# Top-k attention and an MLP mixer on one core: a threshold scaled inside the list pass, a ninth tile's columns copied with its group's, and two smaller moves

## The chip, the cores and the metric

The kernel runs on one core of a Trainium2 chip. The metric is the device time of one execution in microseconds (us). The core has five engines that run side by side, each with its own list of instructions in a fixed order: TensorE (PE, with its weight loads as PEld), VectorE (DVE), ScalarE (ACT), GpSimd (POOL) and SyncE (SP), which here only issues transfers. On one engine an instruction waits for everything ahead of it; between engines they wait on semaphores.

## The reference

For 8 batches and 8 heads, with 576 rows of 64 columns each, attention keeps for each row only the scores that are not below its 32nd largest:

```
scores = scale * q @ k.T                       # 576 x 576 a head
kth    = 32nd largest of each row
scores = where(scores >= kth, scores, -1e9)
attn   = exp(scores - max) / (sum + 1e-9)
x      = attn @ v                              # heads side by side: 576 x 512 a batch
```

Then comes an MLP mixer on each batch: `h = relu(x.T @ w_tok1) @ w_tok2`, `u = x + h.T`, and the output `u + relu(u @ w_ch1) @ w_ch2`.

## The kernel before

**Units.** The work is cut into 32 pairs of heads, counted from 0 (four pairs a batch). A pair has 1152 score rows: nine tiles of 128 rows, where the ninth holds the last 64 rows of both heads. The tiles form two groups, the first of four tiles, the second of five. The columns of a tile are 512 and a tail of 64.

**Scores.** `qk_tr` (L323) transposes q and k on TensorE, `qk_ev` copies them to the tile qkT. `s1_mm` (L358) multiplies for the tail columns of a group's four whole tiles into two PSUM banks (one for each head), and `s1_ev` (L377) copies them to the score tile SS; `s0_mm` and `s0_ev` (L384, L398) do the 512 columns. The ninth tile has its own pair of functions, `st_mm` and `st_ev` (L401, L415), called once for the 512 columns and once for the 64. Nearly all these copies are ScalarE's.

**The 32nd largest.** VectorE finds it group by group, and this is its main work:

- `upper` (L426) takes the larger of columns i and i+288 into `hi`; `split4` (L447) splits these lists again, into `lo` and `hx` (L452, L456, L460).
- four rounds of `top_round` (L465): MAX8 on each tile's list (L473), then MATCH_REPLACE8 (L478, each with a MATCH_VALUE_LOAD) in the first three;
- GpSimd meanwhile makes the list of the smaller elements by integer arithmetic: `both_bits` (L433, an addition) and `lower_bits` (L441, a subtraction), each 128 x 1152 elements;
- **the list pass**, `low_round` (L489): one MAX8 a tile on `lo` (L492), with a TENSOR_REDUCE (L483) behind the first. Its last element of each tile is the threshold, in column KTH+7 of the tile A.

**The mask.** There are two ways. For tiles 0 and 1 of each group ("turned" tiles; none in the last pair's second group), `raise_kth` (L541) scales the thresholds of the whole group by 2^90 into the tile kbig (a TENSOR_SCALAR on VectorE, L544). ScalarE's `steep` (L547) makes from it a tile U that is large below the threshold, GpSimd's `sink` (L556) subtracts U from the scores in SS (L558, two a group), ScalarE's `expo` exponentiates, and a transposing transfer turns the result. For the other tiles ScalarE makes U from the unscaled threshold (`below_act`, L565), and TensorE's transposing products subtract it. In the last pair's second group VectorE masks the tiles itself (`kept`, L572). GpSimd also copies a few columns of A aside for a final check (`keep_ends`, L496, two short copies, L500 and L501), makes the negated maxima (`neg_max`, L515) and issues the loads of v and of the weights.

**The output of attention.** `o_mm` (L644) multiplies the turned probabilities with v and a column of ones; `o_den` (L659) takes the reciprocal of the sums on VectorE (L662); for the second head of odd pairs VectorE multiplies by it at once (`o_ev_dve`, L679, at L681), in the other cases ScalarE does (`o_ev`, L665). Then come the mixer's steps (`h1_mm` to `out_ev`), and for the last batch a longer ending (`plan_part_sums`, `plan_mlp_last`): sums over three quarters of the channels made ahead, kept in free tiles, and joined with the last pair's.

**The order.** No loop nest sets the order. `plan_unit` (L856), `plan_mlp` and the two functions for the last batch give each piece of work to a planner (`Plan`, L40) with an engine, an assumed duration, a priority (often from the table RANK, L20), what it depends on and which buffers it takes. `Plan.order` (L66) plays these through, always starting the task of lowest priority number that is ready, and the instructions are then written in that order on every engine. A task that moves can so shift others. Tasks marked `port` (all of GpSimd's, `upper` and `split4`) exclude each other in the plan; `raise_kth` is not marked. Where TensorE would idle, `spare` (L271) adds multiplications that nothing reads.

In `plan_unit` the scaling is a task of its own behind the list pass:

```python
y = add("FREE", 0.0, 0, lambda: None, deps=[kd[g]])
kb = add("DVE", 0.07, U - 1100, lambda g=g: raise_kth(st, g), deps=[y], acq=[("kbig", u, g)], slack=0.2)
m = add("ACT", 0.67, V + RANK["steep" + str(g)] + i, lambda i=i: steep(st, i), deps=[kb, chain.get("steep")], acq=[("U", u, i)])
```

The zero-length task of the engine "FREE" lets VectorE pick another task first.

Of the kernel before, what the change touches and what calls it, by code (L numbers as in the profile page):

```python
# [19 lines left out]
RANK = {  # L20
    "begin_l": -2054, "o_wait": 16, "t_wait": 6, "q_wait": 272, "v_wait": 112, "pre_mm": -34365, "pre_ev": -31279, "rest_mm": 14920,
    "begin": 31546, "flags": 8794, "rush": -6145, "rush6": -3394, "load": -9078, "qk_tr": 7627, "qk_ev": -3163, "st_mm": -8007,
    "st_ev": 896, "keep": 3463, "h1_mm": -30213, "h1_ev": 3666, "ut_mm": -46945, "ut_ev": -3088, "out_mm": 13329, "out_ev": -772,
# [125 lines left out]
def kernel(  # L149
# [138 lines left out]
    def load_one(st, name, src, b, p, queue=None):  # L288
# [11 lines left out]
        queue.dma_start(  # L300
            out=t[0:TAIL, NT, :, :], in_=rws[:, W:S, :].rearrange("h p c -> p h c")
        )
        st[name] = t
# [41 lines left out]
    def qk_tail_tr(st, kind="tp"):  # L345
        tails = bank(kind)[:, 0 : 2 * TAIL].rearrange("p (i c) -> p i c", i=2)
        for i, name in enumerate("qk"):
            nc.tensor.transpose(
                tails[:, i, :],
                st[name][0:TAIL, NT, :, :].rearrange("p h d -> p (h d)"),  # L350
                identF[0:TAIL, 0:TAIL],
            )
        st["tails"] = tails
# [4 lines left out]
    def s1_mm(st, g, kind="s0"):  # L358
        T = st["T"]
        x = [bank(kind) for hh in range(2)]  # L360
        for a in range(4):
            t, hh = 2 * g + a // 2, a % 2
            nc.tensor.matmul(
                out=x[hh][:, (a // 2) * TAIL : (a // 2 + 1) * TAIL],
                lhsT=T[rows[hh], 0, t * P : (t + 1) * P],
                rhs=T[rows[hh], 1, W:S],
                start=True,
                stop=True,
            )
        st["s1"] = x  # L370
# [30 lines left out]
    def st_mm(st, part):  # L401
        T = st["T"]
        lo, hi = ((0, W), (W, S))[part]
        x = bank("s0")
        for hh in range(2):
            nc.tensor.matmul(
                out=x[hh * TAIL : (hh + 1) * TAIL, 0 : hi - lo],
                lhsT=T[rows[hh], 0, W:S],
                rhs=T[rows[hh], 1, lo:hi],
                start=True,  # L410
                stop=True,
            )
        st["st", part] = x

    def st_ev(st, part):  # L415
        lo, hi = ((0, W), (W, S))[part]
        nc.scalar.copy(out=st["SS", 1][:, 4, lo:hi], in_=st.pop(("st", part))[:, 0 : hi - lo])
# [71 lines left out]
    def low_round(st, g):  # L489
        n, A = 4 + g, st["A", g]  # L490
        for i in range(n):
            nc.vector.max(A[:, i, KTH : KTH + 8], st["lo"][:, i, :])  # L492
            if i == 0:
                both_low(st, g, n - 2, n)

# [44 lines left out]

    def raise_kth(st, g):  # L541
        x = m8p.tile([P, NS], f32, name="kbig", tag="kbig")
        n = 4 + g
        nc.vector.tensor_scalar_mul(x[:, 0:n], st["A", g][:, 0:n, KTH + 7], STEEP)  # L544
        st["kbig", g] = x
# [310 lines left out]
    def plan_unit(u):  # L856
# [6 lines left out]
        for name, src in (("q", q), ("k", k)):  # L863
            aside = u < 2 and name == "k"
            ld[name] = add("ACT" if aside else "SP", 1.75, U - 5000 if aside else U + RANK["load"],
                           lambda name=name, src=src, aside=aside: load_one(st, name, src, b, p, nc.scalar if aside else None),
                           acq=[("ld" + name, u)])
        ev, prev = [], None
        for i in range(2):
            a = add("PE", 0.61, U + RANK["qk_tr"], lambda i=i: qk_tr(st, i), deps=[ld["qk"[i]], prev] + chain.get("first", []), acq=[("tp", u, "q", i)] + ([] if i else [("qkT", u)]), slack=(3.0 if u == 0 else 4.5) if u < 5 else 0.1 * RANK["q_wait"])  # L870
# [18 lines left out]
        for g in range(2):  # L889
            early = u == 0 and g == 0  # L890
            kind = "mps" if early else "s0"
            a = add("PE", 0.65, U + RANK["s_mm" + str(g)] + 10 * g, lambda g=g, kind=kind: s1_mm(st, g, kind), deps=ev + smm[-1:],
# [3 lines left out]
            for hh in range(2):  # L896
                eng = "DVE" if early and hh else "ACT"
                evs.append(
                    add(eng, 0.17, U + RANK["s_ev" + str(g)] + 10 * g, lambda g=g, hh=hh, eng=eng: s1_ev(st, g, hh, eng),
# [15 lines left out]
            if g == 1:  # L915
                for part in range(2):
                    a = add("PE", (1.01, 0.28)[part], U + RANK["st_mm"], lambda part=part: st_mm(st, part),
                            deps=[smm[-1]], acq=[("s0", u, "st", part)],
                            rel=[("qkT", u)] if part else [])
                    smm.append(a)  # L920
                    evs.append(
                        add("ACT", (0.49, 0.12)[part], U + RANK["st_ev"], lambda part=part: st_ev(st, part),
                            deps=[a, e0] + ([evs[-1]] if part else []),
                            rel=[("s0", u, "st", part)])
                    )
# [18 lines left out]
            x = add("DVE", 0.37 * n + 0.08, U + 5 * g, lambda g=g: low_round(st, g), deps=[x, lob])  # L944
# [18 lines left out]
        for g in range(2):  # L963
# [4 lines left out]
            for i in gtiles(g):  # L968
                if i in st["turned"]:
                    if i % 4 == 0:  # L970
                        y = add("FREE", 0.0, 0, lambda: None, deps=[kd[g]])
                        kb = add("DVE", 0.07, U - 1100, lambda g=g: raise_kth(st, g), deps=[y], acq=[("kbig", u, g)], slack=0.2)
                    m = add("ACT", 0.67, V + RANK["steep" + str(g)] + i, lambda i=i: steep(st, i), deps=[kb, chain.get("steep")], acq=[("U", u, i)])
# [45 lines left out]
        for hh in range(2):  # L1019
# [8 lines left out]
            if div:  # L1028
                oe = add("DVE", 0.53, U - 500, lambda hh=hh: o_ev_dve(st, mst, hh, p), deps=[r], rel=[O, ("den", u, hh)])
# [257 lines left out]
    with tc.If(flag != 0):  # L1287
        with tc.For_i(0, B, 1) as bv:
            mst = {}
            for p in range(NPAIR):  # L1290
# [9 lines left out]
                for g in range(2):  # L1300
# [7 lines left out]
                    if g == 1:  # L1308
                        for part in range(2):
                            st_mm(st, part)  # L1310
                            st_ev(st, part)
# [62 lines left out]
```

## Time and profile before

| | us |
|---|---|
| median of 3 runs | 884.5 (884.36 to 884.5) |
| the profiled execution | 884.62 |
| its span, first to last instruction | 882.8 |
| VectorE's first `hi` starts at | 10.53 |
| hi of the second group of pair 31 starts at | 825.62 |
| last MAX8 of the last list pass starts at | 839.57 |

A row of the timeline gives start, duration, engine, line, operation, tile written and tiles read, shapes, and the number of merged instructions. A row of the groups gives the number of instructions, then busy time and the mean duration of one in ns, and the engine's idle time ahead of them. A row of busy times by stretch gives the stretch, its length, the busy time and count on PE, PEld, DVE, ACT and POOL, TensorE's granted clock, the DMA engines' share and GB/s. A row of the waits gives who waited for whom, the total, how often and the longest. The start of one row to the start of the next on the same engine is called a step here: rows overlap, since an instruction may start before the one ahead has fully ended.

### The profile page before, as it was taken

What the parts mean: (1) busy time and instruction counts of PE and PEld (TensorE: products, weight loads), DVE (VectorE), ACT (ScalarE), POOL (GpSimd) and SP (SyncE); (2) the same over time, 40 slices, a digit from 0 to 9 for tenths busy, and PEclk for the clock granted to TensorE, in tenths of its full rate; (3) what the DMA queues carried; (4) which work ended last, traced back from release to release, by engine and by line L of the source; (5) the groups of instructions that cost most, each with busy time, mean ns of one, the idle gap of its engine ahead of it and who ended that gap; (6) DMA issues with size and microseconds to landing.
All of it is one profiled execution on the core that took longest, in us unless ns stands there. A gap on an engine that the chain in (4) does not pass through costs nothing.

```text
span 882.8 us, 22107 instructions
## 1 busy us (share of the span) xinstructions
PE 819.8 (93%) x7328; PEld 468.6 (53%) x7417; DVE 861.7 (98%) x3850; ACT 834.1 (94%) x1857; POOL 597.2 (68%) x513
## 2 busy tenths in 40 slices
PE   8998988999989999999999999899989999899997
PEld 5666545455545555455554555455555455545552
DVE  8999999999999999999999999999999999999993
ACT  4999999999999999999999999999999999999953
POOL 5679776776877766686676777577667767656700
PEclk9999999999999999999999999999999999999999
DMA  9656764254233453226432552224431453111101
GB/s 129 76 93 83 97 96 77 30 86 83 57 59 42 86 84 83 30 42 121 64 58 38 66 110 57 58 38 90 79 77 31 54 110 55 23 32 43 56 19 58
DMA packets 207483, 58.93 MB, mean 67 GB/s; under 512 B 199809, under 2 KB 202305, under 8 KB 207361
## 3 DMA queue, kind: packets, MB, share of 16 engines
q1 hardware_dynamic: 164320, 48.33, 27.2%
q0 software_dynamic: 40560, 8.46, 11.8%
q8 instruction: 60, 0.98, 0.5%
q10 hardware_dynamic: 2480, 0.66, 0.4%
q14 instruction: 63, 0.51, 0.2%
HBM read 35.78 MB, written 9.44 MB: 51 GB/s over the span
## 4 chain that ended last, share of the span: by engine, by line
ACT 52%; DVE 28%; PE 13%; issue 4%; POOL 2%; DMA 1%; SPq 0%; DVEq 0%; ACTq 0%
ACT SS L336 10%; DVE A L473 7%; ACT E L532 7%; DVE hx L478 6%; ACT U L567 6%; ACT U L550 6%; ACT pb L532 5%; PE mps L788 4%; DVE A L492 4%; ACT pt L605 4%; ACT H2T L754 4%; DVE hi L428 3%; ACT xb L672 3%; ACT qkT L336 2%; DVE hx L460 2%
## 5 line engine op out<-in xcount | busy, mean ns | idle before, releaser
L435 POOL TENSOR_TENSOR lo<-SS 128x1152 int32<-128x1152 int32 x64 | 168.8, 2638 | 241.8 <-DVE A L473 178.0
L473 DVE MAX8 A<-hx 128x8 f32<-128x72 f32 (+2 forms) x1152 | 270.1, 294 | 0.0
L478 DVE MATCH_REPLACE8 hx<-A,hx 128x72 f32<-128x72 f32 (+1 forms) x864 | 199.4, 242 | 0.0
L336 ACT COPY SS<-s 128x512 f32<-128x512 f32 x379 | 171.7, 527 | 5.5 <-PE s L389 5.2
L443 POOL TENSOR_TENSOR lo<-lo,hi 128x1152 int32<-128x1152 int32 x64 | 168.7, 2636 | 0.0
L389 PE MATMUL s<-qkT 64*128 64x512 f32 x508 | 161.6, 640 | 0.4 <-ACT SS L336 0.4
L558 POOL TENSOR_TENSOR SS<-SS,U 128x576 f32<-128x576 f32 x126 | 158.6, 1275 | 0.0
L532 ACT ACTIVATE E<-SS,nmax 128x576 bf16<-128x576 f32 x162 | 129.0, 824 | 1.8 <-POOL nmax L518 1.7
L582 PE MATMUL tp<-identB,E 128*128 128x128 bf16 (+1 forms) x785 | 117.4, 221 | 11.0 <-ACT pt L609 7.6
L567 ACT ACTIVATE U<-SS,A 128x576 bf16<-128x576 f32 x157 | 126.7, 837 | 0.0
L585 PE MATMUL tp<-identN,U 128*128 128x128 bf16 (+1 forms) x785 | 112.7, 220 | 9.9 <-ACT U L567 9.0
L492 DVE MAX8 A<-lo 128x8 f32<-128x296 f32 x288 | 116.9, 452 | 0.0
L550 ACT ACTIVATE U<-SS,kbig 128x576 bf16<-128x576 f32 x126 | 100.0, 822 | 4.0 <-DVE kbig L544 4.0
L788 PE MATMUL mps<-wc2b,H2T 128*128 128x512 bf16 (+1 forms) x402 | 101.9, 380 | 1.9 <-issue 1.4
L532 ACT ACTIVATE pb<-SS,nmax 128x576 bf16<-128x576 f32 x126 | 99.5, 814 | 4.2 <-POOL SS L558 4.0
L585 PEld LDWEIGHTS <-U 128*128 128x128 bf16 (+1 forms) x785 | 77.3, 100 | 37.0 <-ACT U L567 20.5
L428 DVE TENSOR_TENSOR hi<-SS 128x1152 f32<-128x1152 f32 x64 | 96.7, 1511 | 0.1
L582 PEld LDWEIGHTS <-E 128*128 128x128 bf16 (+1 forms) x785 | 75.9, 100 | 30.8 <-issue 20.4
L747 PE MATMUL mps<-UT,wc1b 128*128 128x512 bf16 x311 | 80.1, 380 | 6.1 <-ACT H2T L769 2.1
L605 ACT ACTIVATE pt<-tp 128x512 bf16<-128x512 f32 x130 | 79.0, 635 | 2.2 <-PE tp L580 2.2
L389 PEld LDWEIGHTS s<-qkT 64*128 64x128 f32 x508 | 50.5, 185 | 37.3 <-issue 16.4
L650 PEld LDWEIGHTS <-pt 128*128 128x128 bf16 (+1 forms) x1600 | 60.1, 100 | 19.0 <-issue 10.1
(142 smaller groups left out, 1501.2 us busy)
## 6 DMA issues: line engine op xcount, KB each, us to landing
qL<-in_q_dram SPq DMA_DIRECT2D x64, 128.0 KB, 2.7
kL<-in_k_dram SPq DMA_DIRECT2D x60, 128.0 KB, 2.6
out_dram<-ob SPq DMA_DIRECT2D x28, 256.0 KB, 2.1
vb<-in_v_dram POOLq DMA_DIRECT2D x32, 128.0 KB, 4.4
pt<-pb SPq DMA_TRANSPOSE x126, 2.9
wc1b<-in_moe_w_ch_dram POOLq DMA_DIRECT2D x4, 384.0 KB, 5.7
wc2b<-in_moe_w_ch_dram POOLq DMA_DIRECT2D x4, 384.0 KB, 6.0
qL<-in_q_dram SPq DMA_DIRECT2D x32, 32.0 KB, 2.5
```

Of the source, the lines that this page charges most:

```text
L336: nc.scalar.copy(out=out, in_=in_)
L389: nc.tensor.matmul(out=x[:, :], lhsT=T[rows[hh], 0, t * P : (t + 1) * P], rhs=T[rows[hh], 1, 0:W], start=True, stop=True,)
L435: nc.gpsimd.tensor_tensor(out=x[:, 0:4, 0:HALF].bitcast(i32), in0=SS[:, 0:4, 0:HALF].bitcast(i32), in1=SS[:, 0:4, HALF:S].bitcast(i32), op ...
L443: nc.gpsimd.tensor_tensor(out=x, in0=x, in1=st["hi"][:, 0:4, :].bitcast(i32), op=ALU.subtract)
L473: nc.vector.max(A[:, i, at], hx[:, i, 0:w])
L478: nc.vector.match_replace(hx[:, i, 0:w], A[:, i, TOP[r] : TOP[r] + 8], hx[:, i, 0:w], NEG)
L532: nc.scalar.activation(out=x, in_=srow(st, i), func=AF.Exp, bias=st["nmax", g][:, a : a + 1], scale=scale,)
L550: nc.scalar.activation(out=U[:, :], in_=srow(st, i), func=AF.Relu, bias=st["kbig", g][:, a : a + 1], scale=-STEEP,)
L558: nc.gpsimd.tensor_tensor(out=x, in0=x, in1=st["U", i][:, :], op=ALU.subtract)
L567: nc.scalar.activation(out=U[:, :], in_=srow(st, i), func=AF.Relu, bias=kcol(st, i), scale=-1.0)
L582: nc.tensor.matmul(out=out, lhsT=st["E", i][:, cols], rhs=identB[:, :], start=True, stop=False)
L585: nc.tensor.matmul(out=out, lhsT=st["U", i][:, cols], rhs=identN[:, :], start=False, stop=True)
```

## The change

The changed kernel differs in five things.

1. **Ninth tile's last columns.** `s1_mm` of the second group now also multiplies the ninth tile's 64 tail columns, into the first head's bank, and `s1_ev` copies three blocks of 64 columns there in place of two. `st_mm` and `st_ev` keep the 512 columns alone: one ScalarE copy and one PSUM bank fewer in each pair.
2. **Threshold scaled in the list pass.** `raise_kth` and its task are gone; `low_round` scales the turned tiles' thresholds, two columns in place of four or five, ahead of its last MAX8. `steep` now depends on the list pass itself.
3. **A step between reciprocal and scaling.** A task of length zero on "FREE" stands between `o_den` and `o_ev_dve` (but in the last pair), so that VectorE may take another task between them.
4. **First pair's last rows apart.** For pair 0 the last 64 rows of q and k are loaded into the list tile hx, not into the tiles of the other rows. The assumed delay of its loads falls from 3.0 to 2.2 us.
5. **Ranks and durations.** Nearly all numbers in RANK differ, and the assumed durations of the changed tasks are adapted.

The diff, without RANK and without the callers in the repeated computation at the end:

```diff
 def s1_mm(st, g, kind="s0"):
 ...
+        if g:
+            for hh in range(2):
+                nc.tensor.matmul(
+                    out=x[0][hh * TAIL : (hh + 1) * TAIL, 2 * TAIL : 3 * TAIL],
+                    lhsT=T[rows[hh], 0, W:S], rhs=T[rows[hh], 1, W:S], start=True, stop=True,
+                )
 ...
 def s1_ev(st, g, hh, eng="ACT"):
+        n = 3 if g and not hh else 2
         copy(
             eng,
-            s_tile(st, g)[:, hh:4:2, W:S],
-            st["s1"][hh][:, 0 : 2 * TAIL].rearrange("p (a c) -> p a c", a=2),
+            s_tile(st, g)[:, hh : 4 + g : 2, W:S],
+            st["s1"][hh][:, 0 : n * TAIL].rearrange("p (a c) -> p a c", a=n),
         )
 ...
 def low_round(st, g):
         n, A = 4 + g, st["A", g]
+        turned = [i - 4 * g for i in st["turned"] if i in gtiles(g)]
         for i in range(n):
             nc.vector.max(A[:, i, KTH : KTH + 8], st["lo"][:, i, :])
             if i == 0:
                 both_low(st, g, n - 2, n)
+            if i == n - 2 and turned:
+                m = max(turned) + 1
+                x = st["kbig", g] = m8p.tile([P, NS], f32, name="kbig", tag="kbig")
+                nc.vector.tensor_scalar_mul(x[:, 0:m], A[:, 0:m, KTH + 7], STEEP)
 ...
-    def raise_kth(st, g):
-        x = m8p.tile([P, NS], f32, name="kbig", tag="kbig")
-        n = 4 + g
-        nc.vector.tensor_scalar_mul(x[:, 0:n], st["A", g][:, 0:n, KTH + 7], STEEP)
-        st["kbig", g] = x
 ...
+            tail = lists["hx"][0:TAIL, "qk".index(name), 0 : 2 * D].rearrange("p (h d) -> p h d", h=2) if u == 0 else None
 ...
             if div:
-                oe = add("DVE", 0.53, U - 500, lambda hh=hh: o_ev_dve(st, mst, hh, p), deps=[r], rel=[O, ("den", u, hh)])
+                if not last:
+                    r = add("FREE", 0.0, 0, lambda: None, deps=[r])
+                oe = add("DVE", 0.53 if last else 0.43, U - 500, lambda hh=hh: o_ev_dve(st, mst, hh, p), deps=[r], rel=[O, ("den", u, hh)])
```

In RANK, for example, "keep" goes from 3463 to 7959, "pre_mm" from -34365 to -127380, "o_mm0" from 8167 to 12115 and "p_ev1" from -62498 to -51153.

More of the change, by code (lines that the diff above doesn't have):

```diff
@@ L898, in plan_unit @@
                 evs.append(
[L899 removed]
+                    add(eng, 0.22 if g and not hh else 0.17, U + RANK["s_ev" + str(g)] + 10 * g, lambda g=g, hh=hh, eng=eng: s1_ev(st, g, hh, eng),
                         deps=[a] + ([] if early else evs),
@@ L915, in plan_unit @@
             if g == 1:
[L916 to L925, printed above, removed]
+                a = add("PE", 1.01, U + RANK["st_mm"], lambda: st_mm(st), deps=[smm[-1]], acq=[("s0", u, "st")], rel=[("qkT", u)])
+                smm.append(a)
+                evs.append(
+                    add("ACT", 0.49, U + RANK["st_ev"], lambda: st_ev(st), deps=[a, e0], rel=[("s0", u, "st")])
+                )
             n = 4 + g
@@ L943, in plan_unit @@
                     nm = add("POOL", 0.25, U - 1100, lambda g=g: neg_max(st, g), deps=[x])
-            x = add("DVE", 0.37 * n + 0.08, U + 5 * g, lambda g=g: low_round(st, g), deps=[x, lob])
+            x = add("DVE", 0.37 * n + 0.08 + (0.0 if last and g else 0.08), U + 5 * g, lambda g=g: low_round(st, g), deps=[x, lob],
+                    acq=[] if last and g else [("kbig", u, g)])
             chain["low"] = x
@@ L969, in plan_unit @@
                 if i in st["turned"]:
[L970 to L973, printed above, removed]
+                    m = add("ACT", 0.67, V + RANK["steep" + str(g)] + i, lambda i=i: steep(st, i), deps=[kd[g], chain.get("steep")], acq=[("U", u, i)])
                     chain["steep"] = m
@@ L1308 @@
                     if g == 1:
-                        for part in range(2):
-                            st_mm(st, part)
-                            st_ev(st, part)
+                        st_mm(st)
+                        st_ev(st)
                     full_select(st, g)
```

42 lines of the change are left out of this document (18 added, 24 removed), and 10 rows, old and new, of the table RANK.

## The prediction

> **What bounds the kernel now.** I read the page's busy line first, then the engines' busy time by stretch, then VectorE's waits, then VectorE and GpSimd side by side on the timeline, because the line that the change moves (L544) runs on VectorE and its neighbours in time are GpSimd's.
>
> ```profile
> PE 819.8 (93%) x7328; PEld 468.6 (53%) x7417; DVE 861.7 (98%) x3850; ACT 834.1 (94%) x1857; POOL 597.2 (68%) x513
> ```
>
> Three engines are over 90% busy, so shares alone do not tell which one sets the pace.
>
> ```profile
> 300.00:400.00 100.00, 93.92 (x842) 52.42 (x851) 99.86 (x457) 100.00 (x227) 71.86 (x61) 1.00 0.38 64
> 800.00:860.00 60.00, 56.21 (x552) 33.12 (x558) 59.38 (x220) 48.59 (x114) 27.29 (x24) 1.00 0.17 43
> 860.00:883.00 23.00, 16.18 (x79) 6.78 (x79) 7.32 (x13) 7.46 (x14) 0.00 (x0) 0.95 0.16 56
> ```
>
> The columns are PE, PEld, DVE, ACT, POOL. In the middle VectorE and ScalarE both stand at 100%; the last 23 us belong to TensorE.
>
> ```profile
> DVE hx L1199 <- PE s L1156: 6.0, 1, 6.0
> DVE qkT L338 <- PE tp L327: 1.0, 1, 1.0
> ```
>
> VectorE's longest waits lie in the first 10 us and in the last 20; between them none on ScalarE appears. So ScalarE delivers in time and VectorE's own order sets the time from about 10 to 856 us. But VectorE's rows overlap by some 0.08 us (an instruction starts before the one ahead has drained), so "busy" hides short stalls. I therefore count steps, from start to start. Here is the first group of pair 16: its hi, and the end of its list pass up to the next hi; VectorE first, then GpSimd.
>
> ```profile
> 424.93 1.34 DVE L428 TENSOR_TENSOR hi<-SS 128x1152 f32<-128x1152 f32 x1
> ...
> 434.58 0.18 DVE L662 RECIPROCAL rden<-O 128x5 f32<-128x5 f32 x1
> 434.68 0.43 DVE L492 MAX8 A<-lo 128x8 f32<-128x296 f32 x1
> 435.02 0.18 DVE L483 TENSOR_REDUCE lo<-A 128x16 f32<-128x32 f32 x1
> 435.11 1.21 DVE L492 MAX8 A<-lo 128x8 f32<-128x296 f32 x3
> 436.34 0.24 DVE L544 TENSOR_SCALAR kbig<-A 128x4 f32<-128x4 f32 x1
> 436.50 1.73 DVE L428 TENSOR_TENSOR hi<-SS 128x1440 f32<-128x1440 f32 x1
> ```
> ```profile
> 434.04 2.52 POOL L558 TENSOR_TENSOR SS<-SS,U 128x576 f32<-128x576 f32 x2
> 436.50 0.20 POOL L500 COPY ends<-A 128x20 f32<-128x20 f32 x1
> 436.66 1.62 POOL L501 COPY ends<-A 128x10 f32<-128x10 f32 x1
> ```
> ```profile
> L501 POOL COPY ends<-A 128x8 f32<-128x8 f32 x32 | 6.1, 191 | 0.0
> ```
>
> Two things are to be seen. MAX8 and TENSOR_REDUCE run beside GpSimd's two subtractions (L558, ending at 436.56) at their usual lengths. The threshold scaling does not: it ends at 436.58, just after the second subtraction. And L501, 0.19 us in the mean where it stands behind second groups (the last row), here lasts until hi ends, 438.23. The same pattern with other lengths:
>
> ```profile
> 47.26 0.33 DVE L544 TENSOR_SCALAR kbig<-A 128x4 f32<-128x4 f32 x1
> 591.98 0.17 DVE L544 TENSOR_SCALAR kbig<-A 128x4 f32<-128x4 f32 x1
> ```
> ```profile
> 45.05 2.52 POOL L558 TENSOR_TENSOR SS<-SS,U 128x576 f32<-128x576 f32 x2
> 589.60 2.52 POOL L558 TENSOR_TENSOR SS<-SS,U 128x576 f32<-128x576 f32 x2
> ```
>
> Ends: 47.59 against 47.57, 592.15 against 592.12. Its length changes from 0.17 to 0.33 us so that it ends 0.02 to 0.03 us behind the subtraction. This holds at all sixteen places where kbig stands ahead of hi. I conclude: **VectorE's L544 waits until GpSimd's running tensor instruction is over.**
>
> **The change part by part.**
>
> *Threshold scaled in the list pass.* In the built order each of the 63 scalings (now two columns) stands ahead of the last MAX8 of its list pass, not behind the pass. GpSimd's order is the same in both builds, one for one. So I place the new scaling on the old rows. In pair 16's first group the three MAX8 from 435.11 start 0.37 apart (435.11, 435.48, 435.85). The scaling would start at 435.85, with 0.7 us of the second subtraction left; it ends at 436.58 as now. Behind it on VectorE wait the last MAX8 and hi; behind these, ScalarE's threshold passes and GpSimd's both_bits. The last MAX8 then starts where hi starts now, 436.50, and hi one step later, 436.87: +0.37. In return GpSimd's two short copies, now starting with hi, are over before it. Where they are, hi is shorter:
>
> ```profile
> 358.89 1.64 DVE L428 TENSOR_TENSOR hi<-SS 128x1440 f32<-128x1440 f32 x1
> 360.45 0.17 DVE L544 TENSOR_SCALAR kbig<-A 128x4 f32<-128x4 f32 x1
> 360.52 0.45 DVE L452 TENSOR_TENSOR lo<-SS 128x288 f32<-128x288 f32 x1
> ```
>
> 1.64 against 1.73 gives back 0.09. Net +0.28, at sixteen first groups (even pairs, and pair 1): +4.5 us. The wait itself could be anything from 0 to one whole subtraction (2.52 for two, so 1.26); I take the 0.7 that the positions give. That the new scaling is 2 wide and these rows are 4 wide leaves open whether it waits at all: rival B.
>
> [...]
>
> First groups of odd pairs carry the scaling by L681 as well. Pair 17:
>
> ```profile
> 455.58 0.19 DVE L662 RECIPROCAL rden<-O 128x5 f32<-128x5 f32 x1
> 455.81 0.49 DVE L681 TENSOR_TENSOR xb<-O,rden 128x320 bf16<-128x320 f32 x1
> ...
> 461.50 1.20 DVE L492 MAX8 A<-lo 128x8 f32<-128x296 f32 x3
> 462.61 1.64 DVE L428 TENSOR_TENSOR hi<-SS 128x1440 f32<-128x1440 f32 x1
> ```
> ```profile
> 459.85 2.52 POOL L558 TENSOR_TENSOR SS<-SS,U 128x576 f32<-128x576 f32 x2
> ```
>
> *A step between reciprocal and scaling.* L662 to L681 takes 0.23 us, against 0.10 from L662 to an instruction that does not need it (434.58 to 434.68): 0.13 of drain. In the built order MAX8 or MATCH_REPLACE rows now stand between the two at 15 of 16 places, so 0.13 goes, about 1.9 us in all if nothing else ended later. But here the list pass then reaches the scaling at 462.24 − 0.13 = 462.11, the second subtraction ends at 462.37, the scaling at 462.40, the last MAX8 starts at 462.32 and hi at 462.69: 0.08 later than now, and the 0.07 of L544 behind hi (360.45 to 360.52) is saved. Net +0.01; where a second reciprocal left the group (five places), −0.06. Fifteen places: −0.2 us. **The wait eats this gain.**
>
> In second groups (five tiles) the subtractions are over when the list pass reaches the scaling:
>
> ```profile
> 449.23 1.56 DVE L492 MAX8 A<-lo 128x8 f32<-128x296 f32 x4
> 450.71 0.17 DVE L662 RECIPROCAL rden<-O 128x5 f32<-128x5 f32 x1
> 450.80 1.31 DVE L428 TENSOR_TENSOR hi<-SS 128x1152 f32<-128x1152 f32 x1
> 452.04 0.16 DVE L544 TENSOR_SCALAR kbig<-A 128x5 f32<-128x5 f32 x1
> 452.15 0.76 DVE L456 TENSOR_TENSOR lo<-hi 128x576 f32<-128x576 f32 x1
> ```
> ```profile
> 446.70 2.52 POOL L558 TENSOR_TENSOR SS<-SS,U 128x576 f32<-128x576 f32 x2
> ```
>
> GpSimd is done at 449.22, the scaling would come at 450.34. No wait, but today it is free: L456 reads hi, hi ends at 452.11, L456 starts at 452.15, and kbig fills that drain. In the list pass nothing covers it: 31 times 0.07 (bounds 0 and its whole row, 0.16), +2.2 us.
>
> *Reciprocals.* The new ranks move L662. Each in VectorE's open path costs about 0.07 (0.10, less 0.03 that the next MAX8 starts late anyway: 0.34 from 434.68 to 435.02 instead of 0.37). By the built order 13 stand in second groups now and 26 after (+0.9); six stand behind the list pass in even first groups, where they came ahead of it and the subtractions hid them (+0.4); nine cheap ones beside kbig in hi's drain become three (−0.2). Together +1.1.
>
> *Last columns of the ninth tile, one ScalarE copy fewer.*
>
> ```profile
> L417 ACT COPY SS<-s 128x64 f32<-128x64 f32 x32 | 8.3, 261 | 0.0
> ```
>
> 32 rows go and 32 neighbours grow from 128 to 192 columns. TensorE's multiplications stay in number. I take 0: no VectorE wait on ScalarE stands in the open stretch. Were that cover gone, the most it could give is the row's 8.3, the most it could cost nothing.
>
> *First pair's last rows apart, filler, end.* The loads are the same in number and go down the same two queues; the first transpose already waits only for them.
>
> ```profile
> 5.01 0.63 PE L327 MATMUL tp<-identF,qL 128*128 128x128 f32 x4 [0.35 <-DMA qL<-in_q_dram]
> ```
>
> Twelve fewer filler multiplications ahead of it lengthen that idle time and no more: 0, bounds −0.4 and +0.4. SyncE's later stores and transposes change places; VectorE waits for none. At the end ScalarE now takes the part sums' tails before the last pair's UT.
>
> ```profile
> 874.28 2.01 PE L1156 MATMUL tp<-wc2b,H2T 128*128 128x512 bf16 x8
> ```
>
> TensorE's last products end at 876.29, and of the 16.3 us from 860 it is busy 16.18. So I take 0, bounds −1 and +1.
>
> **Sum:** 4.5 − 0.2 + 2.2 + 1.1 = +7.6 us. The profiled execution took 884.62 (span 882.8 and 1.8 around it), the median is 884.5; a difference carries over, giving **892.1**.
>
> **Rivals.** *(B) The two-column scaling does not wait for GpSimd.* For it: no row of that width. Against it: the 4-wide rows. Then even first groups still end with the subtractions (±0), odd ones gain 0.13 fifteen times and 0.07 for five reciprocals fewer (−2.3), second groups lose 2.2 + 0.9: +0.8, or 885.3.
>
> *(C) Faster: the stall at the sixteen places is the scaling's own* (it needs the last MAX8 drained) and goes with it. Its place is the end of even first groups. Its price: hi could start at 436.22 instead of 436.50 and be 0.09 shorter, 0.37 times 16, −5.9; fifteen scalings behind hi −1.1; drains −1.9. Against these 63 times 0.07 = +4.4 and the reciprocals +1.1: −3.4, or 881.1. It decides if hi can start while a subtraction still runs. Against it: hi's start never precedes the second subtraction's end by more than the usual overlap at these places, and L501 stops for the whole of hi.
>
> **How the numbers follow.** Forecast 0.74, B 0.12, C 0.12, the rest 0.02. The forecast's own range is 890 to 895: below, end and start 1.4 and a shorter wait; above, 0.16 instead of 0.07 in second groups (+2.8). To hold 8 in 10 I reach down to B: 885 to 895. A measurement tells about 0.2% (1.8 us) from no change. Slower 0.76, same 0.11 (B), faster 0.13 (C and part of the rest).
>
> **What would show it.** Right: kbig rows in first groups grow to about 0.7 to 0.85 us and end 0.03 behind an L558 row; L501 falls to 0.2 there; hi of 1440 columns is 1.64 throughout; L662 to L681 has no drain; VectorE still has no named wait between 20 and 856. Wrong: kbig rows of 0.16 in first groups (B, and C if even first groups also get shorter than the 11.57 us from 424.93 to 436.50), VectorE waiting on ScalarE, or an end stage that moves by over 1 us.

## The result, and the profile after

The changed kernel takes **897.01 us** in the median of 4 runs (896.2 to 898.07), the kernel before 884.5 (884.36 to 885.15): ratio 1.0136, 95% interval 1.0124 to 1.0149. It is slower, as forecast, but by 12.5 us where 7.6 were forecast, and 897.0 lies above the range of 885 to 895.

In the code after, the line numbers are: hi L429 (was L428), list MAX8 L494 (L492), scaling L500 (L544), short copies L506 and L507 (L500, L501), 512-column scores L396 (L389), part sums' products L1099 (L1103). L558, L662 and L681 keep theirs.

The profiled execution (898.07 us) has a span of 895.9, 13.1 more than before. The page's busy line, the busy times by stretch in the middle, and VectorE's longest waits:

```profile
PE 834.4 (93%) x7426; PEld 468.0 (52%) x7426; DVE 870.5 (97%) x3850; ACT 835.8 (93%) x1825; POOL 569.8 (64%) x513
```
```profile
300.00:400.00 100.00, 93.07 (x819) 51.39 (x818) 99.86 (x454) 99.03 (x221) 65.35 (x57) 1.00 0.40 69
```
```profile
DVE hx L1195 <- PE s L1152: 7.5, 1, 7.5
DVE flagged L1259 <- PE mps L1256: 1.9, 1, 1.9
DVE qkT L338 <- PE tp L327: 1.7, 2, 1.5
DVE SS L338 <- PE s L396: 1.5, 1, 1.5
```

VectorE still sets the pace of the middle: 99.86 busy of 100, and no wait of its own between 20 and 860 us. What is new are waits on TensorE in the first 13 us, and 7.5 in place of 6.0 at the end. So the trace is cut at two rows that both kernels have: the start of the first hi, and of the last pair's second hi. Head, middle and ending, with the ending up to the end of the last instruction of the four computing engines:

| us | head | middle | ending |
|---|---|---|---|
| before | 10.53 | 815.09 | 51.55 |
| after | 13.46 | 824.14 | 52.47 |
| difference | +2.9 | +9.1 | +0.9 |

The forecast had +7.6, all of it in the middle.

**Middle.** The first group of pair 16 again, VectorE and then GpSimd:

```profile
442.27 0.82 DVE L494 MAX8 A<-lo 128x8 f32<-128x296 f32 x2
443.01 0.71 DVE L500 TENSOR_SCALAR kbig<-A 128x2 f32<-128x2 f32 x1
443.64 0.46 DVE L494 MAX8 A<-lo 128x8 f32<-128x296 f32 x1
444.02 1.63 DVE L429 TENSOR_TENSOR hi<-SS 128x1440 f32<-128x1440 f32 x1
```
```profile
441.19 2.51 POOL L558 TENSOR_TENSOR SS<-SS,U 128x576 f32<-128x576 f32 x2
443.65 0.20 POOL L506 COPY ends<-A 128x20 f32<-128x20 f32 x1
443.81 0.18 POOL L507 COPY ends<-A 128x10 f32<-128x10 f32 x1
```

The forecast's signs are here. The scaling, two columns wide, lasts 0.71 us and ends at 443.72, 0.02 behind the second subtraction (443.70). The last MAX8 and hi come behind it. L507 is down to 0.18, and hi at 1.63. In the first groups of even pairs and of pair 1 (17 places) the scaling lasts 0.54 to 0.93 us, in those of odd pairs mostly 0.31 to 0.35, and in second groups 0.14 to 0.15 at 29 of 31 places.

**Head.** TensorE's first products, and behind them the first score products of before:

```profile
5.03 1.09 PE L327 MATMUL tp<-identF,qL 128*128 128x128 f32 x4 [0.87 <-DMA qL<-in_q_dram]
5.91 1.06 PE L327 MATMUL tp<-identF,kL 128*128 128x128 f32 x4
...
8.85 2.02 PE L396 MATMUL s<-qkT 64*128 64x512 f32 x4
10.67 1.92 PE L396 MATMUL tp<-qkT 64*128 64x512 f32 x4
```
```profile
7.72 1.08 PE L389 MATMUL s<-qkT 64*128 64x512 f32 x4
```

The first transposes start when they did (5.03, before 5.01), but four of them take 1.09 in place of 0.63, and four score products 2.02 in place of 1.08. The granted clock of that stretch does not tell it; the last three columns of this row are granted clock, DMA share and GB/s:

```profile
5.00:13.00 8.00, 7.39 (x34) 4.85 (x34) 2.91 (x6) 2.52 (x4) 1.37 (x2) 1.00 1.70 181
```

### The profile page after: what moved, and what is told of

It is laid out like the page before. It is cut to its first block, busy times and chain, and to the rows that moved or that the text cites. A ratio compares the mean times of both kernels' runs of the same rounds, so it can differ in the third digit from the quotient of the medians.

```text
span 895.9 us, 22152 instructions
## 1 busy us (share of the span) xinstructions
PE 834.4 (93%) x7426; PEld 468.0 (52%) x7426; DVE 870.5 (97%) x3850; ACT 835.8 (93%) x1825; POOL 569.8 (64%) x513
## 4 chain that ended last, share of the span: by engine, by line
DVE 53%; ACT 32%; PE 6%; POOL 4%; issue 4%; DMA 0%; SPq 0%; DVEq 0%; ACTq 0%
DVE A L474 14%; DVE hx L479 13%; DVE A L494 7%; ACT SS L336 6%; DVE hi L429 6%; ACT U L550 4%; ACT U L567 4%; ACT E L538 3%; DVE hx L461 3%; DVE lo L457 3%; ACT pb L538 3%; ACT pt L605 2%; DVE hx L457 2%; ACT H2T L754 2%; ACT xb L672 2%
## 5 line engine op out<-in xcount | busy, mean ns | idle before, releaser
L396 PE MATMUL s<-qkT 64*128 64x512 f32 x508 | 161.1, 648 | 1.5 <-ACT SS L336 1.4
L558 POOL TENSOR_TENSOR SS<-SS,U 128x576 f32<-128x576 f32 x126 | 158.6, 1276 | 0.0
L567 ACT ACTIVATE U<-SS,A 128x576 bf16<-128x576 f32 x157 | 124.8, 832 | 0.0
L494 DVE MAX8 A<-lo 128x8 f32<-128x296 f32 x288 | 121.6, 452 | 0.0
L538 ACT ACTIVATE pb<-SS,nmax 128x576 bf16<-128x576 f32 x126 | 102.5, 813 | 9.5 <-POOL SS L558 9.4
L788 PE MATMUL mps<-wc2b,H2T 128*128 128x512 bf16 (+1 forms) x420 | 106.1, 380 | 0.0
L550 ACT ACTIVATE U<-SS,kbig 128x576 bf16<-128x576 f32 x126 | 97.5, 821 | 0.5 <-DVE kbig L500 0.5
L429 DVE TENSOR_TENSOR hi<-SS 128x1152 f32<-128x1152 f32 x64 | 94.7, 1479 | 0.1
L747 PE MATMUL mps<-UT,wc1b 128*128 128x512 bf16 x336 | 82.5, 380 | 7.3 <-ACT H2T L769 4.9
L650 PE MATMUL O<-vb,pt 128*128 128x65 bf16 x1575 | 66.0, 195 | 7.6 <-ACT xb L672 5.9
```

The costliest lines, as they stand in the source:

```text
L396: nc.tensor.matmul(out=x[:, :], lhsT=T[rows[hh], 0, t * P : (t + 1) * P], rhs=T[rows[hh], 1, 0:W], start=True, stop=True,)
L538: nc.scalar.activation(out=x, in_=srow(st, i), func=AF.Exp, bias=st["nmax", g][:, a : a + 1], scale=scale,)
L558: nc.gpsimd.tensor_tensor(out=x, in0=x, in1=st["U", i][:, :], op=ALU.subtract)
L567: nc.scalar.activation(out=U[:, :], in_=srow(st, i), func=AF.Relu, bias=kcol(st, i), scale=-1.0)
```

## The experiments

Theory: the list-pass scaling waits for GpSimd and costs most of it; the head is slow because of the filler that is gone; the ending moves with the plan. Each experiment below compares with runs of the kernel before on the same chip. In the last table stand head, middle and ending of each.

**1. The head.** `spare` fills the idle time that the plan foresees ahead of the first transposes; by the code, the assumed delay of 2.2 in place of 3.0 us (part 4 of the change) leaves 28 multiplications there, not 40. No run changed that delay alone; the number itself is set in `spare`, ahead of the first transposes only (10 for 40 filler multiplications, 7 for 28):

```diff
-        for _ in range(n * 512 // w):
+        for _ in range((10 if at < 6.0 else n) * 512 // w):
```

The changed kernel with 40:

> The changed kernel with 40 filler multiplications ahead of the first transpose, as before, in place of 28; every engine's order is otherwise the changed kernel's. Theory (with 28, TensorE idles so long ahead of the first transposes that it runs its first products at half speed): first hi starts at 10.5 us again, the first four L327 rows take 0.63 in place of 1.09, and the whole is 2.9 us shorter, 894.1. Rival (the slow start comes from the last rows' loads into the list tile): first hi stays at 13.4 and the time at 897.0.

Measured: 894.59 us, ratio 1.0112 (1.0095 to 1.0128); first hi at 10.59. The kernel before with 28:

> The kernel before with 28 filler multiplications ahead of the first transpose in place of 40, nothing else. Theory (the filler alone slows the first products): first hi at 13.4 in place of 10.5, 887.4. Rival (filler costs nothing, as the prediction had it): 884.5, first hi at 10.5 to 10.9.

Measured: 886.66, ratio 1.0018 (1.0009 to 1.0028), first hi at 13.44 in the profiled run. The ten runs reach from 884.62 to 887.55, against 884.72 for the kernel before, so the loss is not the same in each run: from nothing to 2.8.

```profile
0.99 3.17 PE L277 MATMUL mps<-zeros 128*128 128x128 bf16 x28 [0.99 <-DVE zeros L224]
5.00 1.09 PE L327 MATMUL tp<-identF,qL 128*128 128x128 f32 x4 [0.84 <-DMA qL<-in_q_dram]
5.88 1.06 PE L327 MATMUL tp<-identF,kL 128*128 128x128 f32 x4
```

These rows are of the kernel before with 28, and they are those of the changed kernel: the filler alone does it, not the loads into the list tile. Then 24 multiplications, begun later, so that no idle time stands behind them (`zeros` is written after the tiles vb):

> The kernel before with 24 filler multiplications, begun 1.2 us later (their zeros are written after two other tiles), so that they end just ahead of the first transposes. [...] Rival (only the idle time right ahead of the transposes counts): first hi at 10.5 and 884.5.

Measured: 885.15 (884.44 to 887.3, 11 runs), ratio 1.0009 (1.0 to 1.0018), first hi at 11.14.

```profile
2.20 2.74 PE L277 MATMUL mps<-zeros 128*128 128x128 bf16 x24 [2.20 <-DVE zeros L242]
4.91 1.09 PE L327 MATMUL tp<-identF,qL 128*128 128x128 f32 x4
5.79 1.06 PE L327 MATMUL tp<-identF,kL 128*128 128x128 f32 x4
...
7.83 0.66 PE L363 MATMUL mps<-qkT 64*128 64x64 f32 x8 [0.57 <-DVE qkT L338]
```

The author's own estimate was slow transposes and a first hi at 11.5 to 13.5 (885.5 to 887.5), from the shorter work of 24 multiplications (here 2.74 us, against 3.66 for the 40 of before); no run shows that the length of this work alone sets it. Neither this nor the rival is right as stated: the transposes are slow (1.09, before 0.63), but the products from 7.83 on are at full speed (0.66, as in before), at least 4.5 us earlier than with 28 multiplications and a gap (not before 12.4). So the number of multiplications alone does not decide: 24 without a gap cost 0.3 us in the medians, 28 with a gap 1.9. Whether the gap does it, or the later start as well, these runs do not separate.

**2. The scaling in the list pass.** In the changed kernel, with 40 fillers, the four lines of the scaling go behind the loop over MAX8:

> The changed kernel with 40 filler multiplications and with the two-column scaling issued behind the last MAX8 of the list pass, not ahead of it; all other orders as in the changed kernel. Theory (the scaling waits for GpSimd's second subtraction, and what stands behind it on VectorE pays): at the even pairs' first groups hi starts 0.28 to 0.37 earlier than with the scaling inside, second groups keep their 0.07, so 4.5 to 6 us less than the run with 40 fillers alone: 888 to 890. Rival (the place costs nothing, only the scaling's own 0.07 does): the same time as the run with 40 fillers alone.

Measured: 888.01, ratio 1.0037 (1.0023 to 1.0051), 6.6 below the run with 40 fillers alone. A little more than expected. In the kernel before, the scaling goes in, with two columns, and its old task is left empty, so that all other orders are kept:

```diff
             if i == 0:
                 both_low(st, g, n - 2, n)
+            if i == n - 2 and any(t in st["turned"] for t in gtiles(g)): raise_kth(st, g)
```

> The kernel before with the two-column scaling issued ahead of the last MAX8 of each list pass and nothing else moved. Theory (waits for the subtraction): sixteen first groups 0.28 to 0.35 longer (4.5 to 5.6), 31 second groups 0.07 longer (2.2), odd pairs' first groups about even: 891 to 892.5. Rival (no wait for two columns): second groups 2.2 longer, odd first groups the same, sixteen first groups 0: 886 to 887.

Measured: 891.92, ratio 1.0080 (1.0063 to 1.0097). So this part alone costs 7.2 of the 12.5 us. From hi to hi, the 17 first groups of even pairs and pair 1 are 6.3 us longer in all, the 15 of odd pairs 1.7, the 31 second groups 0.7 shorter.

**3. Is it the width?** Two scalings of one column each at the same place, changed kernel with 40 fillers:

```diff
-                nc.vector.tensor_scalar_mul(x[:, 0:m], A[:, 0:m, KTH + 7], STEEP)
+                for c in range(m):
+                    nc.vector.tensor_scalar_mul(x[:, c : c + 1], A[:, c, KTH + 7 : KTH + 8], STEEP)
```

> The changed kernel with 40 filler multiplications, and each scaling of two columns split into two of one column at the same place in the list pass. Compared with the run with 40 fillers and two columns, 894.6. Theory (VectorE's tensor_scalar waits for GpSimd whatever its width): in even pairs' first groups the first one-column row is 0.6 to 0.8 long and ends 0.03 behind L558; the second adds about 0.06 everywhere, 63 times, so 897 to 899. Rival (one column does not take what GpSimd holds): all one-column rows about 0.15, even first groups 0.3 shorter, 63 times 0.06 more: 892 to 894.

Measured: 887.21, ratio 1.0024 (1.0014 to 1.0034), better than even the rival had it. Pair 16's first group, VectorE and GpSimd (lines are one higher here):

```profile
436.88 0.20 DVE L501 TENSOR_SCALAR kbig<-A 128x1 f32<-128x1 f32 x2
436.99 0.46 DVE L494 MAX8 A<-lo 128x8 f32<-128x296 f32 x1
437.37 1.73 DVE L429 TENSOR_TENSOR hi<-SS 128x1440 f32<-128x1440 f32 x1
```
```profile
435.07 2.51 POOL L559 TENSOR_TENSOR SS<-SS,U 128x576 f32<-128x576 f32 x2
```
```profile
L501 DVE TENSOR_SCALAR kbig<-A 128x1 f32<-128x1 f32 x126 | 12.2, 138 | 0.0
```

The same group of rows in the changed kernel:

```profile
L500 DVE TENSOR_SCALAR kbig<-A 128x2 f32<-128x2 f32 x63 | 24.3, 385 | 0.0
```

The subtraction runs until 437.58. Both scalings are over at 437.08, and hi starts at 437.37, ahead of its end. The 126 rows take 0.14 us in the mean, as little as two-column rows of the changed kernel in second groups (0.14 to 0.15 at 29 of 31), against a mean of 0.39 for all 63 two-column rows. The theory that VectorE's scaling waits whatever its width falls: one column does not wait, two columns do, and the four of before did.

**4. Who holds hi?** The kernel before with the scaling on GpSimd (`nc.gpsimd` in L544):

> The kernel before with the scaling on GpSimd in place of VectorE, at the same place of the plan; VectorE's, TensorE's, ScalarE's and SyncE's orders are otherwise those of before. It tells whether hi by itself waits for the second subtraction (the prediction's rival C had it that hi could start earlier once no scaling stands ahead of it). Theory (hi waits by itself): hi of even pairs' second groups still starts no more than 0.1 ahead of the second subtraction's end, and the time is 884 to 885, or a little more where GpSimd's scaling delays its next addition. Rival C (the scaling alone held hi back): 16 times 0.2 to 0.28 less, 880 to 881.5.

Measured: 893.68, ratio 1.0117 (1.0079 to 1.0155), so neither. GpSimd's rows at pair 16:

```profile
438.93 2.52 POOL L558 TENSOR_TENSOR SS<-SS,U 128x576 f32<-128x576 f32 x2
441.40 1.64 POOL L500 COPY ends<-A 128x20 f32<-128x20 f32 x1
...
443.50 0.77 POOL L544 TENSOR_SCALAR kbig<-A 128x4 f32<-128x4 f32 x1
```
```profile
L544 POOL TENSOR_SCALAR kbig<-A 128x4 f32<-128x4 f32 x32 | 88.1, 2753 | 6.6 <-DVE A L492 5.4
```

On GpSimd the 4-wide scaling takes 2.75 us in the mean, 0.77 here, against 0.21 (205 ns) on VectorE before, and GpSimd's next work is late by that. As to its question, VectorE's row there:

```profile
441.12 1.85 DVE L428 TENSOR_TENSOR hi<-SS 128x1440 f32<-128x1440 f32 x1
```

The subtraction ends at 441.45, so hi's row does start early; it ends at 442.97, 1.52 behind. Then two one-column scalings where the kernel before has its wide one:

```diff
-        nc.vector.tensor_scalar_mul(x[:, 0:n], st["A", g][:, 0:n, KTH + 7], STEEP)
+        for c in range(2): nc.vector.tensor_scalar_mul(x[:, c : c + 1], st["A", g][:, c, KTH + 7 : KTH + 8], STEEP)
```

> The kernel before with each scaling of four or five columns replaced by two of one column at the same place; all orders are otherwise those of before. Theory (one column does not wait for GpSimd; hi then stands waiting inside its own row until the second subtraction is over, and ends 1.52 behind it in place of 1.68): 16 times 0.16 less, and 0 to 0.06 more at the 47 places in hi's drain: 882 to 884.7, hi of even pairs' second groups starting 0.1 to 0.3 ahead of the subtraction's end. Rival (the gain is lost again behind hi): 884.7 or above.

Measured: 883.72, ratio 0.9990 (0.9981 to 0.9999).

```profile
435.52 0.20 DVE L544 TENSOR_SCALAR kbig<-A 128x1 f32<-128x1 f32 x2
435.63 1.72 DVE L428 TENSOR_TENSOR hi<-SS 128x1440 f32<-128x1440 f32 x1
```
```profile
433.32 2.51 POOL L558 TENSOR_TENSOR SS<-SS,U 128x576 f32<-128x576 f32 x2
```

hi starts 0.20 ahead of the subtraction's end (435.83) and ends at 437.35, 1.52 behind it. So it was with one column in the list pass: 437.37 + 1.73 = 439.10, 1.52 behind 437.58. The earlier hi starts, the longer its row, and the end stays at the same distance from the subtraction's: with the scaling on GpSimd hi started 0.33 ahead (441.12 against 441.45), lasted 1.85 and ended 1.52 behind as well. Before, hi at 436.50 ended 1.67 behind it. What differs is GpSimd's short copy L500: before, it ran its 0.20 us first; with one column it lasts until hi is over, as in the run on GpSimd. Here is its row:

```profile
435.79 1.64 POOL L500 COPY ends<-A 128x20 f32<-128x20 f32 x1
```

**5. The other parts.** The ninth tile's columns alone, on the kernel before:

> The kernel before with the ninth tile's last columns multiplied and copied with its group's, nothing else (the planner moves some reciprocals by itself). Theory (ScalarE's 32 short copies are covered): 884.7, between 884 and 885.5. Rival (VectorE does wait on ScalarE somewhere, or the end gains): 882 to 883.5. Other rival (the larger copy makes the ending later, as in the changed kernel): 885.8, with the time from the last hi to the end 1 us longer.

Measured: 887.24, ratio 1.0034 (1.0018 to 1.0049). The middle is 0.4 longer, the ending 1.1, as the other rival had it; the whole is 2.1 longer. The step between reciprocal and scaling alone:

> The kernel before with the step between reciprocal and scaling alone. Theory (the drain of 0.13 at 15 places can be saved, but the planner now writes the threshold scaling ahead of hi in most of these groups, where it costs its 0.07 and waits for GpSimd's subtraction): odd pairs' first groups 0 to 1 us less in all, 884 to 885. Rival (the drain is saved and nothing is given back): 1.9 less, 882.8.

Measured: 889.73, ratio 1.0060 (1.0047 to 1.0074). The middle is 0.3 shorter, as expected, but the ending 4.4 longer, which neither side had. In the last stretch a reciprocal of pair 30 moves from 833.59 to 839.59, and with it all that leads to the part sums; that reciprocal, the first part sums (L1105 here, L1103 before) and the last pair's second product with v, here first, then before:

```profile
839.59 0.17 DVE L662 RECIPROCAL rden<-O 128x5 f32<-128x5 f32 x1
```
```profile
833.59 0.19 DVE L662 RECIPROCAL rden<-O 128x5 f32<-128x5 f32 x1
```
```profile
844.43 2.36 PE L1105 MATMUL mps<-UT,wc1b 128*128 128x512 bf16 x9
...
855.09 1.06 PE L650 MATMUL mps<-vb,pt 128*128 128x65 bf16 x25
```
```profile
839.90 2.29 PE L1103 MATMUL mps<-UT,wc1b 128*128 128x512 bf16 x9 [0.25 <-ACT UT L737]
...
851.43 1.06 PE L650 MATMUL mps<-vb,pt 128*128 128x65 bf16 x25
```

The changed kernel (40 fillers) with the ranks of before, and then without the scaling in the list pass:

> The changed kernel with 40 filler multiplications and with the RANK table of before. Compared with the run with 40 fillers and the new ranks, 894.6. Theory (the new ranks cost through the places of the reciprocals, 1.0, and through the ending, 1.1): 892.5, and the time from the last hi to the end as before. Rival (both come from the other parts of the change): 894.6 and the ending 1.1 longer still.

> The changed kernel with 40 filler multiplications and with the scaling as a task of its own behind the list pass, four or five columns, as before; new ranks, ninth tile and the step between stay. Theory (what is left of the change costs the ending's 1.0 and the reciprocals' 1.1): 886 to 887.5. Rival (the rest of the change is worth something once the scaling is out): 883 to 884.7.

Measured: 896.13, ratio 1.0134 (1.0117 to 1.0151), and 889.8, ratio 1.0057 (1.0042 to 1.0072). Both theories fell; in the first run the rival is nearer. The old ranks leave the middle as it is (823.31 against 823.40) and lengthen the ending by another 1.8; without the list-pass scaling the ending is 4.1 longer than before. Each change of the task list gives the planner another ending.

**6. Combinations.** One-column scalings with the step between, then the step for the early batches alone, so that the last groups' reciprocals keep their places:

> The kernel before with one-column scalings in place of the wide ones and with the step between reciprocal and scaling. Theory (without the wait, the drain that the step saves is kept): 1.0 to 1.9 less than with the one-column scalings alone, 881 to 883. Rival (the step moves other work and gives the gain back): the same as the one-column scalings alone or above.

> The kernel before with one-column scalings in place and with the step between reciprocal and scaling for batches 0 to 4 alone, so that the plan of the last pair's groups has its reciprocals where before has them. Theory (the step gains in the middle and its loss of 4.4 lies in the ending, which the plan of the last batches sets): time from the last hi to the end 51.5 to 52.0, the middle 0.5 to 1.2 shorter than with one column alone, 882.3 to 883.5. Rival (the step's loss goes with the step wherever it stands): 885 or more.

> The same with the step for batches 0 and 1 alone. Theory: the ending as before, the middle 0.1 to 0.5 shorter than with one column alone, 883.2 to 883.7. Rival: 885 or more.

Measured: 886.76, ratio 1.0025 (1.0016 to 1.0034); 882.97, ratio 0.9981 (0.9972 to 0.9990); 884.16, ratio 0.9990 (0.9981 to 0.9999). With the step everywhere the middle is 1.1 shorter than with one column alone, and the ending takes back 4.4. With the step up to batch 4 the ending is that of before, and this version, the best of all, beats the kernel before by 0.2%. Its profiled run (884.11) is the longest of its eleven and shows a middle only 0.2 shorter than with one column alone, so what the step adds to the one column is not settled. With the step in batches 0 and 1 alone, the middle is that of one column alone, not the 0.1 to 0.5 shorter one that was expected.

Differences to the kernel before; the first column is of medians, the other three of the profiled runs, as in the first table. The heads of +0.3 to +0.8 in runs with 40 fillers are read as a later turn of TensorE to full speed in that execution (last section), not as the edit's. Rows show it for two of them: the 40 fillers took 4.45 us with the scaling behind the pass (+0.4) and with one column in the pass of the changed kernel (+0.8), against 3.66 in before:

| run | us | head | middle | ending |
|---|---|---|---|---|
| changed kernel | +12.5 | +2.9 | +9.1 | +0.9 |
| with 40 fillers | +9.9 | +0.1 | +8.3 | +0.9 |
| before, 28 fillers | +1.9 | +2.9 | -0.2 | 0.0 |
| before, 24 late fillers | +0.3 | +0.6 | 0.0 | 0.0 |
| changed, 40, scaling behind the pass | +3.3 | +0.4 | +1.4 | +0.9 |
| before, scaling in the pass | +7.2 | +0.1 | +7.3 | -0.1 |
| changed, 40, one column | +2.0 | +0.8 | +0.8 | +1.3 |
| before, scaling on GpSimd | +8.5 | +0.5 | +6.5 | +2.2 |
| before, ninth tile alone | +2.1 | +0.7 | +0.4 | +1.1 |
| before, step alone | +5.2 | 0.0 | -0.3 | +4.4 |
| changed, 40, old ranks | +11.0 | 0.0 | +8.2 | +2.7 |
| changed, 40, without list pass | +5.3 | +0.3 | +1.6 | +4.1 |
| before, one column | -0.8 | 0.0 | -1.4 | 0.0 |
| the same, step everywhere | +2.2 | +0.4 | -2.5 | +4.4 |
| the same, step in batches 0 to 4 | -1.9 | +0.7 | -1.6 | +0.2 |
| the same, step in batches 0 and 1 | -0.7 | +0.6 | -1.4 | 0.0 |

## Why the prediction was wrong

- **VectorE sets the time of the middle**: right.
- **The scaling waits for GpSimd's second subtraction**: right, and right in size. The terms 4.5 - 0.2 + 2.2 = 6.5 are this part; alone on the kernel before it cost 7.2. The working took hi's gain of 0.09 off the first groups; counted from hi to hi it lies in the second groups, as do the rows saved in hi's drain. That two columns wait as four do was shown by no row of before; in the changed kernel 28 scalings of two columns end 0.02 to 0.03 us behind the subtraction. Pair 0's scaling is long as well (0.54 from 24.32), but the MAX8 behind it starts at 24.38: in the changed kernel nothing is held up there.
- **"The wait eats this gain"** (of the step between): right. In the changed kernel no VectorE scaling follows its reciprocal directly but in the last pair, and pair 17's list pass reaches its scaling earlier and waits there:

```profile
469.58 0.31 DVE L500 TENSOR_SCALAR kbig<-A 128x2 f32<-128x2 f32 x1
469.80 0.46 DVE L494 MAX8 A<-lo 128x8 f32<-128x296 f32 x1
470.18 1.63 DVE L429 TENSOR_TENSOR hi<-SS 128x1440 f32<-128x1440 f32 x1
```
```profile
467.35 2.51 POOL L558 TENSOR_TENSOR SS<-SS,U 128x576 f32<-128x576 f32 x2
```

  0.31 us to 469.89, behind L558's end at 469.86. hi starts 0.32 behind it in odd pairs as in even ones (470.18; 444.02 against 443.70): the group's end is now GpSimd's plus one MAX8. Odd pairs' first groups are longer by 1.6 in all in the changed kernel with 40 fillers, which has the step, and by 1.7 with the scaling in the pass alone, which has not. Without the wait (one column) the step everywhere shortened the middle by 1.1, in one pair of profiled runs; up to batch 4 it shortened it by 0.2.
- **Reciprocals, +1.1**: the size fits what is left of the middle (8.3 with 40 fillers, less 7.3: 1.0), but the reason given, the new ranks, does not: with the old ranks the middle is the same. The other edits move the reciprocals anyway: 23 stand in second groups with the old ranks, 20 with the ninth tile alone and 22 with the step alone, against 13 before and 26 in the changed kernel. That they cost the 1.0 no run shows by itself. The 9.1 of the changed kernel's own profile is 0.7 more, mostly in three groups of that one execution.
- **The step that failed: "Twelve fewer filler multiplications ahead of it lengthen that idle time and no more: 0, bounds −0.4 and +0.4."** They cost 2.4 us in the medians (897.01 - 894.59; 2.6 when each run is taken against its own runs of before), 2.9 in the profiled run. The filler had been read as work of no use, and the 0.35 of idle time behind it as all that fewer of them could lengthen. What the runs show is that with 40 TensorE is at full speed before the transposes or soon behind their start, and the four score products behind them take 1.08 us; with 28 they take 2.02. Without these 2.4 the time lies within the range, if barely (894.59).
- **The end, "I take 0, bounds −1 and +1"**: +0.9, within its bounds but taken as 0. In the trace of after, the two heads of the last pair are multiplied in the other order, VectorE's scaling (0.49) comes first and ScalarE's longer one (1.11) last, and TensorE's L692 for the last pair waits 1.02 and starts 28.6 us behind the last hi, before 27.7 (the last row):

```profile
864.78 1.11 ACT L672 ACTIVATE xb<-O,rden 128x64 bf16<-128x64 f32 x5 [2.94 <-DVE rden L662]
```
```profile
866.19 0.72 PE L692 MATMUL mps<-xb,w1b 128*128 128x128 bf16 x10 [1.02 <-ACT SS L1109]
```
```profile
853.35 0.73 PE L692 MATMUL mps<-xb,w1b 128*128 128x128 bf16 x10
```

  The scaling is over at 865.89; what ended the wait is ScalarE's copy of the part sums' tails right behind it (L1109); the prediction had seen these copies move and taken it as 0. This is read from the rows; no run changed that order alone. That the bounds were too narrow is shown: other plans gave +1.1 to +4.4 there.
- **Ninth tile, "I take 0"**: its copy is covered in the middle (alone: +0.4), but its tasks moved the ending by 1.1.
- **Rival B** (no wait for two columns) is out: 0.71 us rows. **Rival C** had half of it: once no wide scaling stands ahead of it, hi does start while a subtraction runs (0.20 us ahead of its end). But it ends 1.52 behind that end all the same, so each place is worth about 0.15 (hi's end from 1.67 to 1.52 behind the subtraction), not 0.37; the 17 first groups became 2.1 us shorter, not 5.9.

## What to carry to other kernels

Filler ahead of the first products is not idle work: before its number is cut, look whether the products behind it are at full speed (here 1.08 us with 40, 2.02 with 28), and repeat the run, since the loss differs from run to run (here from nothing to 2.8 us). An instruction that waits for another engine holds up all that stands behind it on its own engine: moved ahead of work that could have run during the wait, it pushes that work behind the wait's end (here a two-column scaling ahead of the last MAX8, up to 0.93 us long and 7.2 us in the whole). Where it waits beside another engine's work, a narrower form may not (here one column, 0.14 in the mean, in place of two, 0.39). And a plan that is replayed as a whole changes the ending with any task: price it by its own chain (reciprocal, ScalarE, TensorE), not by "TensorE is busy".

## What the runs showed of the hardware

**Two-column and one-column scalings differ.** Scalings of 128x4 on VectorE (before, 16 places) end 0.03 to 0.04 us behind the running GpSimd subtraction, those of 128x2 (changed kernel) 0.02 to 0.03 behind it at 28 of 31 places; at the other three one or both of GpSimd's short copies went ahead as well, and the scaling ended 0.2 to 0.33 behind the subtraction. 126 of 128x1, at the same places, take 0.14 in the mean, and at pair 16 both were over 0.50 us ahead of the subtraction's end. Why one column differs from two no run here shows.

**hi can start beside a subtraction, and its row is then longer.** hi starts 0.2 to 0.33 us ahead of the subtraction's end in the rows shown, and is the longer for it: 1.72 to 1.85 where it takes 1.64 alone. It ends 1.52 behind in each of them.

**TensorE's first products run at half speed, and the turn to full speed is not at a fixed time.** The 40 fillers took 3.66 us in the profile of before and 4.45 in another:

```profile
0.99 4.45 PE L277 MATMUL mps<-zeros 128*128 128x128 bf16 x40 [0.99 <-DVE zeros L224]
5.24 1.06 PE L327 MATMUL tp<-identF,qL 128*128 128x128 f32 x4
6.09 0.92 PE L327 MATMUL tp<-identF,kL 128*128 128x128 f32 x4
6.94 0.34 PE L348 MATMUL s<-identF,hx 64*128 64x64 f32 x2
```

These are of the run with one column in the list pass: all 40 are slow and most of the transposes, and full speed comes between 6.1 and 6.9. In before, the fillers start 0.107 us apart until 3.71 and 0.056 apart behind it, so the turn lies at about 3.7, and all transposes take 0.63 a row. The fillers took 3.89 us in the changed kernel with 40 and 4.33 in before with the scaling in the pass. Over the 14 profiled runs with 40 fillers the first hi lies between 10.5 and 11.3. So the turn wanders between runs of the same 40 fillers. With 28 fillers and a gap of 0.87 (changed kernel) the turn did not come before 12.4. With 3.17 us of filler and a gap of 0.84 behind it (before with 28) nine of ten runs took 1.2 to 2.8 us more than the median of before. The turn came 2.7 us after the first filler in before and over 5 us after it in the run with one column; what sets it no run here shows. The granted clock of the profile stood at 1.00 from 0 to 13 us in before and in the changed kernel, so here the rows' own lengths are the sign, not that column.
